# An attention and two-MLP kernel on one core: weight conversions on GpSimd's DMA queue, and new due times for VectorE and ScalarE

## The chip, the cores and the metric

The kernel runs on one core of a Trainium2 chip. The metric is the device time of one execution in microseconds. Three runs of the kernel before gave 1081.07, 1081.65 and 1086.11, so its median is 1081.65 us.

## The reference

Three layers, one behind the other; the second and third act on 1792 tokens of 768 values.

```
q, k, v: (4, 12, 448, 64) fp32
scores = q @ k.T / 8 - log(448);  attn = sigmoid(scores);  x = attn @ v   -> (1792, 768)
h = x @ w_in (768 x 2048, float64);   x = (h * cos(h)) @ w_out (2048 x 768, float64)
g = x @ w_gate; val = x @ w_val (768 x 1536, float64);  out = (silu(g) * val) @ w_out2
```

The weights arrive as float64 words. The kernel converts each 128 x 768 block to fp32 on the chip and keeps the result in a scratch buffer in DRAM (`swi`, `swo`, `swg`, `swv`, `swd`).

## The kernel before, in words

*Precision.* Every fp32 operand of a matmul is split into a high half (a rounded copy, made by ScalarE, sometimes by VectorE) and a low half (the difference, made by VectorE). Each product is three matmuls: high by high, high by low, low by high.

*Attention.* 24 pairs of heads run one after another. For each, VectorE splits q and k (L723, L724), TensorE makes four chunks of scores (24 matmuls, L734), ScalarE takes the sigmoid of each chunk out of PSUM (L738), and TensorE multiplies by v (16 matmuls, L748). ScalarE copies the result to `r` (L750). SP's queue loads `rqk` (q and k) and `vs` (v).

*The two MLPs.* The work is cut into 28 units: 16 of layer 1 (two halves of the tokens times eight blocks of 256 hidden values) and 12 of layer 2. A stage is one layer for one half of the tokens; units 0 to 7 are stage 0, 8 to 15 stage 1, 16 to 21 stage 2, 22 to 27 stage 3. An up product of a unit is done in seven block products of 9 matmuls, numbered 1 to 7 (`seven`, L1000), instead of eight, so the operands are sums and differences of blocks of x and of the weights, and the results are put together from PSUM banks by VectorE (`sum22`, `sum12`) and ScalarE (`first_copy`, `second_copy`, `fifth`). Layer 2 has two such products in a unit, gate and value. For layer 1, `h_cos_h` then makes a scaled copy and a rounded copy on ScalarE, takes their difference on VectorE (L816, the rounding step), the sine on ScalarE and the product on VectorE. `split_g` makes the two halves of g. Six down products of 12 matmuls (L902) follow, in the middle of the next unit's seven. At a stage's start the seven operands of x are made anew from `r` (`inputs`): a difference for four of them, a high half (L658 on ScalarE, L660 on VectorE) and a low half.

*Conversions.* One conversion loads the float64 words (`raw`, beside attention `lr`), and takes one or two ScalarE and four or five VectorE instructions; the result (`lt` beside attention, later `t` or `cv`) is stored. Four sets of buffers are lent to conversions while attention runs (`lend_pool`). All of these DMAs are issued by SP, in the order in which the planner gives them.

*What sets the order.* The order on TensorE is a string of tokens for each unit: a digit is a block product, d is a down product of the unit before. The order on the other engines is laid while the program is built, by a planner (`Order`). Each step says which engines can do it and how long it takes, and may carry a due time; the planner advances a clock, picks of the ready steps the one that can start first, and among equals the one with the smallest due time. Due times are the planned time of the product that needs the result, less a number of microseconds. Attention's own instructions are written in program order, and `beside` fills their gaps with planned steps. On the chip only the order is kept: each engine runs its list in sequence and waits on semaphores. Most VectorE and ScalarE instructions are recorded at the line of a helper (L230, L227).

Of the kernel before, what the change touches and what calls it, by code (L numbers as in the profile page):

```python
# [11 lines left out]
I32 = mybir.dt.int32  # L12
# [3 lines left out]
ALU = mybir.AluOpType  # L16
# [25 lines left out]
LATENCY = 0.15  # L42

# [30 lines left out]
class Order:  # L74
# [51 lines left out]
    def run(self, until=math.inf):  # L126
        while self.ready:
# [11 lines left out]
            (start, _), task, engine, time = best  # L139
            if start >= until:  # L140
                return
# [9 lines left out]
def block_kernel(  # L151
# [85 lines left out]

    LANDING = 5.0
    PAIR = 5.8
# [16 lines left out]
    PRODUCT = 0.203  # L256

    FIRST = ("1562734", "15627dd3dd4dd")
    ONE = ("1526dd7d3d4dd", "15d2d6d7d3d4d")
    TWO = "15d26d73d4"  # L260
    LAST = ('1526d734', '15d26d73d4dd')
# [116 lines left out]
    for n, (layer, _, c) in enumerate(units):  # L378
        for i in range(2):
# [4 lines left out]
            for w, key in of:  # L384
                uses.setdefault((id(w), 2 * c + i), due[key] - 25.0)
    todo = iter(todo)

    def lend_pool():
# [3 lines left out]
        for a in range(4):  # L392
# [3 lines left out]
            order.spawn(conversions(raw, t, backs[-1], stop), end)  # L396
# [11 lines left out]

    def absolute(t, words):
# [7 lines left out]
        return {"ACT": 0.9, "DVE": 0.58}, do  # L417

    def conversions(raw=None, t=None, back=None, stop=None):

        while not stop:
# [6 lines left out]
            yield move(raw.rearrange("p n two -> p (n two)"), flat(w[f]).bitcast(I32))  # L428
            yield LANDING
# [5 lines left out]
            yield by(time, ({"DVE": 0.56}, lambda _: nc.vector.tensor_scalar(  # L435
                t, t, HI_MOST, HI_LEAST, op0=ALU.min, op1=ALU.max
            )))
            yield {"DVE": 0.56}, lambda _: nc.vector.tensor_scalar(
                ti, ti, 3, 0x3FFFFFF8, op0=ALU.logical_shift_left, op1=ALU.bitwise_and
            ), time  # L440
            yield {"DVE": 0.96}, lambda _: nc.vector.scalar_tensor_tensor(
# [3 lines left out]
            yield by(time, vec(0.97, ti, ti, raw[:, :, 0], ADD))  # L445
# [4 lines left out]
            yield move(there[0], t)  # L450
# [55 lines left out]
    def operands():  # L506
# [16 lines left out]
        def lower(keys, s, t, lo, hi, size, room, free, done):  # L523
            yield by(due[keys[0]] - 1.2, vec(0.16 + size / 950, lo, t, f32(hi), SUB))
# [39 lines left out]
        def split(keys, t, free=None):  # L564
# [4 lines left out]
            yield by(due[keys[0]] - 2.4, copy(0.2 + size / 1200, hi, t))  # L569
# [19 lines left out]
        for n in range(n_units):  # L589
# [10 lines left out]
            for u in range(units[n][0]):  # L600
# [6 lines left out]
                yield combine(sums, a21, a22, ADD, due[n, u, 5] - 3.0)  # L607
                yield combine(a21, a11, a21, SUB, due[n, u, 7] - 3.0)
                last_sums = yield from split([(n, u, 5)], sums)
                yield first  # L610
                yield combine(a11, sums, a11, SUB, due[n, u, 6] - 4.0)
                yield combine(a12, a12, a11, SUB, due[n, u, 3] - 4.0)
# [32 lines left out]
    def inputs(s):  # L645
# [9 lines left out]
        def to_hi(out, t):  # L655
# [5 lines left out]
            return {"ACT": 1.32, "DVE": 0.9}, do  # L661
# [5 lines left out]
        def operand_of(i):  # L667
            t, parts = make[i]
            time = due[n, 0, i]
            if parts:  # L670
                for event in after[i]:
                    yield event
                yield by(time - 5.0, vec(1.6, t, parts[0], parts[1], SUB))
                made_t[i].set()
# [5 lines left out]
            yield by(time - 3.2, to_hi(hi, t))  # L680
# [443 lines left out]
```

## Time and profile before

| | |
|---|---|
| profiled execution | 1087.36 us |
| its span, first to last instruction | 1085.3 us |
| runs | 1081.07, 1081.65, 1086.11 us |
| TensorE matmuls busy | 1065.9 us (98%) |
| VectorE busy | 848.9 us (78%) |
| ScalarE busy | 664.8 us (61%) |
| GpSimd busy | 124.7 us (11%), 97 instructions |
| mean granted TensorE clock | 0.992 |

Busy shares are of the span. DMA issues are not counted as busy. Attention fills the span to about 154 us, layer 1 from there to about 600 us, layer 2 the rest. The profiled execution took 5.7 us more than the median of the runs.

### The profile page before, as it was taken

What the parts mean: (1) busy time and instruction counts of PE and PEld (TensorE: products, weight loads), DVE (VectorE), ACT (ScalarE), POOL (GpSimd) and SP (SyncE); (2) the same over time, 40 slices, a digit from 0 to 9 for tenths busy, and PEclk for the clock granted to TensorE, in tenths of its full rate; (3) what the DMA queues carried; (4) which work ended last, traced back from release to release, by engine and by line L of the source; (5) the groups of instructions that cost most, each with busy time, mean ns of one, the idle gap of its engine ahead of it and who ended that gap; (6) DMA issues with size and microseconds to landing.
All of it is one profiled execution on the core that took longest, in us unless ns stands there. A gap on an engine that the chain in (4) does not pass through costs nothing.

```text
span 1085.3 us, 14759 instructions
## 1 busy us (share of the span) xinstructions
PE 1065.9 (98%) x5507; PEld 933.1 (86%) x5507; DVE 848.9 (78%) x1138; ACT 664.8 (61%) x1005; POOL 124.7 (11%) x97
## 2 busy tenths in 40 slices
PE   9999999999999899999997999999999999999998
PEld 5554569999989799999997999999999999999997
DVE  4969759989999999989899888897559644555643
ACT  6887768877777777777776665554345344433330
POOL 0000002001111101100023100111111210110100
PEclk9999999999999899999998999999999999999999
DMA  9999424545654145454513565655122322112002
GB/s 267 301 264 248 143 88 146 200 150 175 220 202 146 59 161 205 160 188 146 189 59 122 170 221 202 203 189 175 45 73 76 117 85 73 56 48 73 30 1 102
DMA packets 64455, 156.68 MB, mean 144 GB/s; under 512 B 10112, under 2 KB 36736, under 8 KB 64384
## 3 DMA queue, kind: packets, MB, share of 16 engines
q1 hardware_dynamic: 64240, 155.51, 45.3%
q8 instruction: 43, 0.70, 0.3%
q10 hardware_dynamic: 144, 0.23, 0.1%
q14 instruction: 28, 0.23, 0.1%
HBM read 123.47 MB, written 32.24 MB: 143 GB/s over the span
## 4 chain that ended last, share of the span: by engine, by line
PE 88%; DVE 9%; issue 1%; ACT 1%; DMA 0%; DVEq 0%; ACTq 0%
PE banks L1000 42%; PE banks L902 33%; PE banks L748 7%; PE banks L734 6%; DVE x L230 2%; DVE r L230 2%; DVE u L230 1%; DVE g L230 1%; DVE wa L230 1%; DVE wb L230 0%; DMA rqk<-in_qk 0%; DVE u L816 0%; DVE s L230 0%; DVE x L660 0%; ACT x L658 0%
## 5 line engine op out<-in xcount | busy, mean ns | idle before, releaser
L902 PE MATMUL banks<-g,wb 128*128 128x448 f32 x1044 | 224.2, 362 | 1.1 <-ACT g L227 0.6
L1000 PE MATMUL banks<-x,wb 128*128 128x448 f32 x1044 | 224.9, 363 | 0.3 <-ACT banks L227 0.3
L902 PEld LDWEIGHTS banks<-g,wb 128*128 128x128 f32 x1044 | 195.5, 187 | 15.5 <-ACT g L227 1.4
L1000 PEld LDWEIGHTS banks<-x,wb 128*128 128x128 f32 x1044 | 196.8, 189 | 14.0 <-ACT banks L227 0.7
L902 PE MATMUL banks<-g,wa 128*128 128x448 f32 x720 | 160.6, 370 | 9.8 <-ACT g L227 8.5
L1000 PE MATMUL banks<-x,wa 128*128 128x448 f32 x738 | 159.7, 362 | 0.1
L902 PEld LDWEIGHTS banks<-g,wa 128*128 128x128 f32 x720 | 137.9, 192 | 21.3 <-ACT g L227 9.3
L1000 PEld LDWEIGHTS banks<-x,wa 128*128 128x128 f32 x738 | 138.2, 187 | 10.3 <-issue 0.7
L227 ACT ACTIVATE u<-u 128x448 f32<-128x448 f32 x179 | 99.4, 570 | 39.4 <-DVE u L230 26.6
L230 DVE TENSOR_TENSOR u<-u,banks 128x448 f32<-128x448 f32 x119 | 73.4, 617 | 57.1 <-PE banks L1000 54.1
L230 DVE TENSOR_TENSOR r<-banks,r 128x896 f32<-128x896 f32 (+1 forms) x69 | 74.2, 1075 | 50.5 <-PE banks L902 50.0
L738 ACT ACTIVATE a<-banks 128x896 f32<-128x896 f32 x96 | 82.9, 920 | 20.2 <-PE banks L734 12.4
L230 DVE TENSOR_TENSOR wb<-t,wb 128x768 fp32r<-128x768 f32 x73 | 69.5, 956 | 14.9 <-ACT wb L227 14.4
L227 ACT ACTIVATE g<-u 128x448 fp32r<-128x448 f32 x97 | 55.1, 572 | 39.0 <-DVE u L230 23.9
L1000 PE MATMUL banks<-x,s 128*128 128x448 f32 x360 | 78.5, 362 | 0.0
L734 PEld LDWEIGHTS banks<-qk 64*128 64x128 f32 x576 | 51.5, 188 | 29.6 <-ACT a L738 8.2
L227 ACT ACTIVATE wb<-t 128x768 fp32r<-128x768 f32 x73 | 60.9, 837 | 24.6 <-PE banks L1000 17.8
L512 POOL TENSOR_TENSOR sum<-t 128x384 f32<-128x384 f32 x20 | 35.2, 1758 | 339.9 <-DMA t<-swi 78.1
L734 PE MATMUL banks<-qk 64*128 64x448 f32 x576 | 69.9, 386 | 3.5 <-ACT a L738 2.2
L227 ACT ACTIVATE r<-banks 128x896 f32<-128x896 f32 x52 | 47.8, 920 | 41.1 <-PE banks L902 41.0
L1000 PEld LDWEIGHTS banks<-x,s 128*128 128x128 f32 x360 | 67.5, 188 | 4.5
L227 ACT ACTIVATE banks<-banks 128x448 f32<-128x448 f32 x80 | 42.3, 529 | 46.3 <-PE banks L1000 45.1
(103 smaller groups left out, 1476.3 us busy)
## 6 DMA issues: line engine op xcount, KB each, us to landing
raw<-in_w_out SPq DMA_DIRECT2D x23, 768.0 KB, 5.2
t<-swi SPq DMA_DIRECT2D x32, 384.0 KB, 3.2
t<-swo SPq DMA_DIRECT2D x64, 192.0 KB, 2.5
rqk<-in_qk SPq DMA_DIRECT2D x47, 224.0 KB, 7.5
raw<-in_w_gate SPq DMA_DIRECT2D x12, 768.0 KB, 4.6
raw<-in_w_val SPq DMA_DIRECT2D x12, 768.0 KB, 4.9
t<-swg SPq DMA_DIRECT2D x18, 384.0 KB, 3.0
t<-swd SPq DMA_DIRECT2D x34, 192.0 KB, 3.0
```

The lines of the kernel that those rows point to most:

```text
L227: return {"ACT": time}, lambda _: nc.scalar.activation(**kw)
L230: return {"DVE": time}, lambda _: nc.vector.tensor_tensor(out=out, in0=in0, in1=in1, op=op)
L512: on.tensor_tensor(out=out, in0=a, in1=b, op=op)
L734: nc.tensor.matmul(sc[:, j], lhsT=both[half, m, 1, starts[c]:starts[c] + P], rhs=both[half, p, 0], start=n == 0, stop=n == 2,)
L738: nc.scalar.activation(out=a, in_=sc, func=AF.Sigmoid, bias=-math.log(S), scale=1.0 / math.sqrt(D))
L748: nc.tensor.matmul(o[half], lhsT=value, rhs=a[:, j], start=c == 0, stop=c == NCH)
L902: nc.tensor.matmul(banks[:, first + e - d, :N], lhsT=w[:, m, e % KH, :], rhs=g[:, 1 - p], start=(i, m, p) == (0, 0, 0) and is_fresh and no ...
L1000: nc.tensor.matmul(bank, lhsT=w[:, m, k, :], rhs=x[p][:, k], start=(k, m, p) == (0, 0, 0) and i in (1, 5), stop=(k, m) == (KH - 1, 1), ski ...
```

## The change

Beside attention, the raw weights are loaded and the converted ones stored by GpSimd's queue (`move_beside`) instead of SP's. Each of the four lent conversions first waits a planned 6.0 + 4.5 a microseconds (a from 0 to 3), and then for a one-column copy on GpSimd that reads the q and k of pair a + 1, so that its first load is issued behind those. The planner allows 9.5 us for landing there instead of 5.0.

All leads before due times stand in one table now, with new values; the planned durations of the conversions, of the low halves and of the x casts on VectorE (0.9 to 1.55) are new, and a VectorE step that starts while GpSimd is planned busy counts 1.12 times its duration. The token strings of layer 2 (TWO) and of the last unit (LAST) differ; those of layer 1 do not.

```diff
+LEAD = {
...
+    "ghi": -2.87,
+    "glo": -2.34,
...
+    "xlo": -11.72,
...
+            if engine == "DVE" and self.busy.get("POOL", 0.0) > start:
+                time *= 1.12
...
+    def move_beside(out, in_):
+        return {"POOL": 0.9}, lambda _: nc.gpsimd.dma_start(out=out, in_=in_)
+
     LANDING = 5.0
+    LANDING_BESIDE = 9.5
...
-    TWO = "15d26d73d4"
-    LAST = ('1526d734', '15d26d73d4dd')
+    TWO = '1526dd7d34'
+    LAST = ('1562734d', '1d5627dd3dd4')
...
+    def begun(a, raw_qk, steps):
+
+        yield 6.0 + 4.5 * a
+        yield {"POOL": 0.3}, lambda _: nc.gpsimd.tensor_copy(warm[:, a:a + 1], raw_qk[:, (a + 1) % 4, 1, S - 1:S])
+        yield from steps
...
-            yield move(raw.rearrange("p n two -> p (n two)"), flat(w[f]).bitcast(I32))
-            yield LANDING
+            convey = move_beside if back else move
+            yield convey(raw.rearrange("p n two -> p (n two)"), flat(w[f]).bitcast(I32))
+            yield LANDING_BESIDE if back else LANDING
...
-            yield by(due[keys[0]] - 1.2, vec(0.16 + size / 950, lo, t, f32(hi), SUB))
+            yield by(due[keys[0]] - LEAD["wlo"], vec(0.25 + size / 1080, lo, t, f32(hi), SUB))
...
-            return {"ACT": 1.32, "DVE": 0.9}, do
+            return {"ACT": 1.32, "DVE": 1.55}, do
...
-            yield by(time - 1.7, vec(1.6, lo, t, f32(hi), SUB))
+            yield by(time - LEAD["xlo"], vec(1.6, lo, t, f32(hi), SUB))
...
-        yield by(time - 1.5, copy(0.6, g[:, 1], f))
-        yield by(time - 0.8, vec(0.65, g[:, 0], f, f32(g[:, 1]), SUB))
+        yield by(time - LEAD["ghi"], copy(0.6, g[:, 1], f))
+        yield by(time - LEAD["glo"], vec(0.65, g[:, 0], f, f32(g[:, 1]), SUB))
...
```

Three places in the order. First VectorE at the end of unit 15, the last of layer 1. Before, from the accumulation behind `sum12` on: `r1<-banks` is that accumulation, `x1<-r0` low halves of the next stage's operand, `r0<-r0` a difference for it, L816 the rounding step of unit 15.

```order
L230 TENSOR_TENSOR r1_65<-banks_63,r1_65 128x896
L230 TENSOR_TENSOR x1_1325<-r0_64,x1_1325 128x3x448 x2
L230 TENSOR_TENSOR r0_64<-r0_64 128x1344
L816 SCALAR_TENSOR_TENSOR u0_1440<-u5_1449,u0_1440 128x448
L230 TENSOR_TENSOR x1_1325<-t3_1450,x1_1325 128x768
L230 TENSOR_TENSOR wb2_1448<-t_66,wb2_1448 128x768
L816 SCALAR_TENSOR_TENSOR u2_1442<-u5_1449,u2_1442 128x448
L230 TENSOR_TENSOR wa0_68<-t_66,wa0_68 128x768
```

The same place now, from `sum12` (the first row) on; L858 is the rounding step, `g3<-u1` and `g1<-u4` are the low halves of g for the first down product.

```order
L261 TENSOR_TENSOR u1_1436<-u1_1436,u0_1435 128x448
L858 SCALAR_TENSOR_TENSOR u4_1439<-u5_1444,u4_1439 128x448
L261 TENSOR_TENSOR x0_72<-r0_64,x0_72 128x3x448
L261 TENSOR_TENSOR u3_1438<-u3_1438,banks_63 128x448
L261 TENSOR_TENSOR r0_64<-r0_64 128x1344
L261 TENSOR_TENSOR u4_1439<-u4_1439,u2_1437 128x448
L261 TENSOR_TENSOR wb2_1443<-t_66,wb2_1443 128x768
L261 TENSOR_TENSOR g3_1434<-u1_1436,g3_1434 128x448
L261 TENSOR_TENSOR r0_64<-r0_64 128x1344
L261 TENSOR_TENSOR wa0_68<-t_66,wa0_68 128x768
L261 TENSOR_TENSOR g1_1432<-u4_1439,g1_1432 128x448
L261 TENSOR_TENSOR x0_72<-r0_64,x0_72 128x3x448
```

The rounding step and the halves of g moved ahead of low halves of x; those stand behind g now.

Second, VectorE in the middle of layer 1, behind the seven of unit 4. Before, with L816 the rounding steps of groups (1, 1), (0, 1) and (1, 0) of unit 4, and `wa1` the low half of a weight pair.

```order
L816 SCALAR_TENSOR_TENSOR u1_1441<-u5_1449,u1_1441 128x448
L230 ISA t_66<-raw1_1434,t_66 128x1536
L816 SCALAR_TENSOR_TENSOR u0_1440<-u5_1449,u0_1440 128x448
L230 TENSOR_TENSOR u1_1441<-u1_1441,u4_1444 128x448
L816 SCALAR_TENSOR_TENSOR u2_1442<-u5_1449,u2_1442 128x448
L414 TENSOR_SCALAR cv_1435<-raw0_1433 128x768
```

The same place now, from the rounding step of group (0, 1) to that of group (1, 0); `wa1` and `wa0` are low halves of weight pairs.

```order
L858 SCALAR_TENSOR_TENSOR u2_1437<-u5_1444,u2_1437 128x448
L261 TENSOR_TENSOR wa1_69<-t3_1445,wa1_69 128x768
L261 TENSOR_TENSOR g0_1431<-u0_1435,g0_1431 128x448
L261 TENSOR_TENSOR wa0_68<-t_66,wa0_68 128x768
L858 SCALAR_TENSOR_TENSOR u4_1439<-u5_1444,u4_1439 128x448
```

Two low halves of weights and a low half of g moved between the two rounding steps.

Third, the DMAs beside attention. Before, on SP's queue: `lr` are raw weights, `swi0<-lt0` the store of a converted block, `rqk` and `vs` the inputs of attention.

```order
L236 DMA lr3_120<-in_w_in 128x1536
L707 DMA rqk_79<-in_qk 64x2x448 x2
L708 DMA vs4_165<-in_v 128x384
L716 DMA t_66<-in_v 64x3x64 x2
L707 DMA rqk_79<-in_qk 64x2x448 x2
L708 DMA vs5_217<-in_v 128x384
L236 DMA swi0_261<-lt0_115 128x768
L707 DMA rqk_79<-in_qk 64x2x448 x2
```

On GpSimd's queue now, with the one-column copies (L447).

```order
L447 COPY warm_71<-rqk_79 128x1
L270 DMA lr3_120<-in_w_in 128x1536
L270 DMA swi0_313<-lt0_115 128x768
L270 DMA lr0_114<-in_w_out 128x1536
L270 DMA swi1_381<-lt1_117 128x768
L270 DMA lr1_116<-in_w_out 128x1536
```

SP's queue keeps `rqk`, `vs` and the loads of converted weights; the loads of raw weights and the stores beside attention moved to GpSimd's.

## Rows read from the trace of the kernel before

**Rows 1.** The chain that ended last, shares of the span by engine.
```profile
PE 88%; DVE 9%; issue 1%; ACT 1%; DMA 0%; DVEq 0%; ACTq 0%
```
**Rows 2.** TensorE's waits: engine, line, releaser: us in total, times, longest.
```profile
PE banks L902 <- ACT g L227: 9.1, 3, 5.7
PE banks L734 <- ACT a L738: 2.2, 1, 2.2
```
**Rows 3.** A window: us, busy time of each engine, granted clock, DMA share, GB/s.
```profile
365.20:371.80 6.60, 6.01 (x15) 5.00 (x16) 5.21 (x7) 3.27 (x6) 2.00 (x1) 0.50 0.55 173
```
**Rows 4.** The chain in order of time, layer 1: start us, us, what.
```profile
275.37 7.20 PE banks L1000 x36
...
392.49 7.20 PE banks L1000 x36
```
**Rows 5.** Timeline of TensorE in attention: start us, us, engine, line, operation, [idle before].
```profile
91.11 2.48 PE L748 MATMUL banks<-a,vs 128*64 128x448 f32 x12
...
104.48 0.87 PE L734 MATMUL banks<-qk 64*128 64x448 f32 x6 [2.19 <-ACT a L738]
105.28 4.17 PE L748 MATMUL banks<-a,vs 128*64 128x448 f32 x12
```
**Rows 6.** Timeline of TensorE at the switch from stage 0 to stage 1.
```profile
365.19 0.74 PE L902 MATMUL banks<-g,wa 128*128 128x448 f32 x1 [2.80 <-ACT g L227]
366.52 4.47 PE L902 MATMUL banks<-g,wa 128*128 128x448 f32 x11 [0.59 <-DVE g L230]
```
**Rows 7.** Timeline of TensorE at the switch from layer 1 to layer 2.
```profile
572.65 2.56 PE L902 MATMUL banks<-g,wb 128*128 128x448 f32 x12
...
583.45 1.97 PE L1000 MATMUL banks<-x,s 128*128 128x448 f32 x9
...
600.27 1.36 PE L902 MATMUL banks<-g,wa 128*128 128x448 f32 x6
```
**Rows 8.** Timeline of VectorE at the switch from layer 1 to layer 2.
```profile
574.63 0.61 DVE L230 TENSOR_TENSOR u<-u,banks 128x448 f32<-128x448 f32 x1
575.16 1.55 DVE L230 TENSOR_TENSOR x<-r,x 128x1344 fp32r<-128x1344 f32 x1
576.63 1.08 DVE L230 TENSOR_TENSOR r<-banks,r 128x896 f32<-128x896 f32 x1
577.63 3.01 DVE L230 TENSOR_TENSOR x<-r,x 128x1344 fp32r<-128x1344 f32 x2
...
582.03 0.61 DVE L816 SCALAR_TENSOR_TENSOR u<-u,u 128x448 f32<-128x448 f32 x1
...
583.44 0.95 DVE L230 TENSOR_TENSOR wb<-t,wb 128x768 fp32r<-128x768 f32 x1
...
591.25 0.61 DVE L230 TENSOR_TENSOR g<-u,g 128x448 fp32r<-128x448 f32 x1
```
**Rows 9.** Timeline of ScalarE in attention.
```profile
92.19 0.92 ACT L738 ACTIVATE a<-banks 128x896 f32<-128x896 f32 x1 [0.32 <-PE banks L748]
...
101.86 1.32 ACT L658 ACTIVATE x<-r 128x1344 fp32r<-128x1344 f32 x1 [2.84 <-DVE r L230]
```
**Rows 10.** Timeline of VectorE in attention.
```profile
74.92 0.63 DVE L723 CAST qk<-rqk 128x896 fp32r<-128x896 f32 x1 [3.93 <-DMA rqk<-in_qk]
```
**Rows 11.** Timeline of VectorE and TensorE behind unit 4.
```profile
282.39 0.62 DVE L230 TENSOR_TENSOR g<-u,g 128x448 fp32r<-128x448 f32 x1
282.41 3.78 PE L902 MATMUL banks<-g,wb 128*128 128x448 f32 x18
```
**Rows 12.** DMA issues to 130 us: count, KB each, median us to landing.
```profile
rqk<-in_qk SPq DMA_DIRECT2D x47, 224.0 KB, 7.5
lr<-in_w_in SPq DMA_DIRECT2D x8, 768.0 KB, 9.7
```
**Rows 13.** Timeline of GpSimd at the switch from layer 1 to layer 2.
```profile
588.35 6.66 POOL L512 TENSOR_TENSOR sum<-t 128x384 f32<-128x384 f32 x1 [17.93 <-DVE u L816]
```
**Rows 14.** A group of the page's part 5: busy us, mean ns, idle before.
```profile
L512 POOL TENSOR_TENSOR sum<-t 128x384 f32<-128x384 f32 x20 | 35.2, 1758 | 339.9 <-DMA t<-swi 78.1
```

More of the change, by code (lines that the diff above doesn't have):

```diff
@@ L42 @@
 LATENCY = 0.15
+LEAD = {
+    "u": 6.41,
+    "f": 3.86,
+    "stt": 4.78,
+    "sin": 3.9,
+    "mult": 4.38,
+    "ghi": -2.87,
+    "glo": -2.34,
+    "whi": 17.07,
+    "wlo": 7.63,
+    "c5": 3.74,
+    "c7": -12,
+    "c6": -0.3,
+    "c3": -12,
+    "xd": 4.51,
+    "xhi": 11.35,
+    "xlo": -11.72,
+    "sv": -9.73,
+    "acc": -11.08,
+    "bank": -3.13,
+    "first": -1.99,
+    "second": 1.43,
+    "fifth": -1.94,
+    "s22": 4.84,
+    "s12": 4.53,
+    "silu": -12,
+    "conv": 19.63,
+}
 class Event:
@@ L395, in lend_pool @@
             backs.append(order.event())
-            order.spawn(conversions(raw, t, backs[-1], stop), end)
+            order.spawn(begun(a, raw_qk, conversions(raw, t, backs[-1], stop)), end)
         def swap():
@@ L444, in conversions @@
             ), time
-            yield by(time, vec(0.97, ti, ti, raw[:, :, 0], ADD))
+            yield by(time, vec(1.0, ti, ti, raw[:, :, 0], ADD))
             if not back:
@@ L449, in conversions @@
             there[0] = dram.tile([P, KD * P], F32, tag=f"s{names[id(w)]}{f}", name=f"s{names[id(w)]}{f}")
-            yield move(there[0], t)
+            yield convey(there[0], t)
             order.spawn(landed(there[1], None if back else t), 0)
@@ L764, in attention @@
             split(0)
-            stops = [lend_pool()]
+            stops = [lend_pool(raw_qk)]
             for i in range(NPAIR):
@@ L846, in accumulate @@
         two, acc = banks[:, first:first + 2, :N], R[h][:, j, d:d + 2]
-        time = after_down(n, j, d) - 1.3
+        time = after_down(n, j, d) - LEAD["acc"]
         if place[n, j, d] == len(down_steps) - 1:
@@ L876, in banker @@
                     acc = R[units[n][1]][:, j, d:d + 2]
-                    yield by(due["down", n, j, d] - 1.3, copy(0.92, banks[:, first:first + 2, :N], acc))
+                    yield by(due["down", n, j, d] - LEAD["bank"], copy(0.92, banks[:, first:first + 2, :N], acc))
                 held[j, d] = first
@@ L968, in after @@
                     z[ij] = ((yield tmps), order.event())
-                order.spawn(silu(z[ij][0], h, read, z[ij][1], min(time, due["g", n, key[2]] - 6.0)), 0)
+                order.spawn(silu(z[ij][0], h, read, z[ij][1], min(time, due["g", n, key[2]] - LEAD["silu"])), 0)
             else:
```

54 lines of the change are left out of this document (27 added, 27 removed).

## The prediction

> **What bounds the kernel now.** I read the chain that ended last first [rows 1]. Its shares by engine are to be read as one statement: 88% is TensorE's own matmuls, so the kernel is a TensorE stream and only what interrupts that stream costs time. Then TensorE's waits [rows 2]: the matmuls of the down products (L902) wait for ScalarE's half of g, 9.1 us in 3 waits, the longest 5.7; attention's scores (L734) wait once, 2.2 us. Waits alone are not the price, since the granted clock falls after a long one: it stands at 0.50 (1.2 GHz instead of 2.4) in the stretch behind the wait at 365 us [rows 3]. So I price each interruption by the position of the products behind it.
>
> From 572.65 to 583.45 TensorE runs 54 matmuls (12 + 9 + 24 + 9) in 10.80 us without a wait: 0.200 us a matmul [rows 7], and 27.0 us for the 135 of a whole unit of layer 1.
> - A, attention at 102 us: 2.19 us idle, then 16 matmuls in 4.17 us where twelve of them normally take 2.48 [rows 5]: 2.19 + 1.69 = 3.9 us.
> - B, units 4 to 7: from 275.37 to 392.49 are 117.12 us for four units of 27.0, so 9.1 us lost [rows 4]. Of these the switch from stage 0 to stage 1 takes 2.80 + 0.59 idle, 4.47 - 11 x 0.2 = 2.3 at half clock, and about 0.5 to the end of that stretch: 6.2 us [rows 3, 6]. The other 2.9 us lie inside units.
> - C, the switch from layer 1 to layer 2: from 583.45 to 600.27 are 16.82 us for 9 + 12 + 18 = 39 matmuls, 7.8 us undisturbed: 9.0 us lost [rows 7].
>
> Together 22.0 us. With the profiled execution at 1087.36 us, a stream without any of it would take 1065.3.
>
> **Why those waits are there.** C first. Between the last sum of unit 15 (574.63) and the first rounding step of its h cos h (582.03) VectorE does three low halves of the next stage's operand x (one, then two in 3.01 us), an accumulation and a difference for x; the last low half of g that TensorE waits for starts at 591.25 [rows 8]. The work of the next stage stands ahead of the work that TensorE needs first. B's switch has the same form. A is a ScalarE cast of a stage operand that sits in front of the next pair's sigmoids and waits 2.84 us for a VectorE difference [rows 9]; VectorE was late because it had waited for q and k, 3.93 us in front of 74.92 [rows 10].
>
> **The change part by part.** *Stage switches.* The order shows, for unit 15, the rounding step directly behind the sum, and low halves of x behind it. I add up the rows from that sum to the last low half of g that the first down product reads, with durations start to start from the same stretch (u or g step 0.53, x step 1.47, accumulation 1.00, and 0.87 for the low half of a weight pair, which is what 582.03 to 583.44 leaves behind a u step [rows 8]): 19 rows and 16.6 us before, 14 rows and 11.7 us after, 4.9 us less; for unit 7, 16 rows and 13.7 us before, 11 rows and 9.0 us after, 4.7 us less. At unit 7 the wait was 3.4 us, so it goes. At unit 15 the wait was 5.7 us, so 0.8 would stay; but layer 2's new token string puts two more products (18 x 0.2 = 3.6 us) in front of the first down product of unit 15, so it goes too. What is late next is product 6 of unit 16: its low half of x moves from 1 row behind the sum to 15 rows, 13.2 us. TensorE has 14.4 us of products between (one down, product 4, two downs, products 1, 5, 2), and in the trace the sum started 2.0 us behind the end of product 3 (574.63 against 572.65, where the next down product began [rows 7, 8]): 14.4 - 2.0 - 13.2 = -0.8, so a wait of 0.8, bounds 0 to 1.5. Gain 6.2 + 9.0 - 0.8 = 14.4 us.
>
> *Inside the units.* VectorE's order there hardly changes in length: over the 16 units of layer 1 the rows from the last sum to g's last low half of group (1, 0) are 295 before and 291 after. One place gets worse. In unit 4 the rounding step of that group falls behind both low halves of a weight pair: 7.9 us of rows ahead of it become 9.7, and the low half of g comes 0.9 to 1.7 us later. Before, that low half started at 282.39 and the down product at 282.41 [rows 11], so there is no margin to speak of. I take 1.5 us of new wait and keep the 2.9 us. Bounds: 0, if the finer spacing also removes the old 2.9, to 9, if each of three such places costs 3 with its stretch at half clock. The waits of 2.19 and 2.80 us had stretches at half clock behind them [rows 3, 5, 6]; whether one of 1.5 has, no row shows, and that lies in these bounds.
>
> *Attention.* 12 conversions instead of 13 run beside it; their 12 loads and 12 stores leave SP's queue for GpSimd's. On SP a load of q and k no longer stands behind a store that waits for VectorE. Before, q and k took 7.5 us at the median and the raw weights 9.7 in one queue [rows 12]. The cast that made A has the same form after: it stands behind the last sigmoid of pair 14 and needs the VectorE difference behind the split of pair 15. Its slot opens when that sigmoid ends, at about 93.1 before [rows 9]. Back from there over VectorE's rows after: difference 1.5, split 1.6, two x steps 2.9, split 1.6, four conversion steps and a cast 4.2, split 1.6, conversion steps 3.2, split 1.6, so the split of pair 12 has to start by about 74.9; before it started at 74.92 and had waited 3.93 us for q and k [rows 10]. With these loads out of the weights' way it should start earlier, so A goes: 3.9 us, bounds 0 to 3.9. The planner also counts VectorE's x casts at 1.55 us instead of 0.9, which is what an x step of that size takes [rows 8].
>
> What GpSimd's queue costs is not in this trace: no DMA is issued there. From below it is nothing; from above, one GpSimd addition took 6.66 us beside a busy VectorE, while its group's mean is 1.76 [rows 13, 14]. 24 issues are 42 us at the mean, or 160 us at the worst, in some 120 us. I take the mean, the nearest thing to an issue whose writes share time with VectorE: hidden, since the first cast of raw weights stands behind the sigmoids of pair 2 now and of pair 1 before, and the loads keep the margin that 9.7 us of landing had there. If that cover is gone, rival 2 gives the price.
>
> The Trainium skill speaks against this edit: "SBUF — State Buffer", section "SBUF: two separate sides", says that a DMA issued from GpSimd's queue needs GpSimd to write its descriptors, and that VectorE in a two-port mode locks it out until its instruction ends. By that rule an issue waits at most for one VectorE instruction at a time; the 6.66 us row agrees that GpSimd can be held off, and no run so far shows a descriptor held off.
>
> *Rest.* 11 weight sums move from VectorE to GpSimd (89 to 100 there), 19 us at 1.76 [rows 14]; VectorE gives up about 11 x 0.53 = 6 us over 900, off the path. Layer 2's and the end's new strings keep every matmul; layer 2 ran without waits worth naming before, so I cost them at nothing, with VectorE's idle time there as cover.
>
> **Sum.** 1087.36 - 3.9 - 14.4 + 1.5 = 1070.6 for an execution like the profiled one. The median of the runs is 1081.65, 5.7 below it, and the runs reach from 1081.07 to 1086.11. If they lose less to the same waits, the new kernel is near 1070; if the gap is one of the measurement, at 1064.9. I take 1068.
>
> **Rivals.** (1) *The waits move into the units.* The copies of g are now 4.4 and 3.1 us less urgent. If 8 of 16 units each lose 1.5 us, the sum is 12 - 1.5 = 10.5 higher than mine, 1078 to 1081: no change. For it: VectorE's load and the missing margin at 282.4; against it: the row counts are level.
>
> (2) *GpSimd's queue is too slow, slower than before.* Place: the casts of raw weights that ScalarE does once per pair, in order, in front of the sigmoids; a late load stops the scores. Price: 24 issues of t us must fit into 120. From t = 5.0 on, what exceeds it lands on TensorE; 14 us of gain are eaten at t = 5.6 and at 6.66 the kernel takes about 1107. For it: the 6.66 row. Against it: the 1.76 mean. A milder form, first weights late by 20 us in all, gives 1088. (3) *Attention is not mended*, because the same cast waits for the same kind of difference: 1072. Against it: the earlier q and k.
>
> **How the numbers follow.** Half a per cent (5.4 us) is about what a measurement of this kernel can tell from no change: faster means under 1076.2. Forecast with the waits at the switches gone: 0.62 around 1068, own range 1063 to 1073; rival 3 about 0.14, also faster; rival 1 0.14, mostly no change; rival 2 0.10, slower. So 0.76 faster, 0.14 the same, 0.10 slower. The range ends at 1062, below 1064.9 by the 2.9 us that may also go, and at 1079, inside rival 1.
>
> **What would show it.** Right: TensorE's timeline gapless around 365 and 591 us, no granted clock of 0.50 there, and the rounding step of unit 15 directly behind its sum; in attention no wait of L734's successor for ScalarE, and VectorE's waits for q and k below 3 us. Wrong: waits of about 1 to 2 us for g in many units of layer 1, a wait in front of product 6 behind the switch above 2 us, or ScalarE's cast of raw weights waiting for a DMA in attention.

## The result and the profile after

Four runs of the changed kernel took 1069.14, 1069.96, 1070.30 and 1070.52 us, a median of 1070.13; the kernel before stands at 1081.62 over four. The ratio is 0.9883 with a 95% interval of 0.9856 to 0.9911: faster by 1.2%. The prediction said 1068 and gave 1062 to 1079. The profiled execution took 1069.14 us, with a span of 1067.4.

The chain that ended last, in the kernel after, shares of the span by engine:

```profile
PE 92%; DVE 5%; issue 1%; ACT 1%; DMA 0%; DVEq 0%; ACTq 0%
```

Against [rows 1], 4% of the span went from VectorE to TensorE in that chain. TensorE's waits in the kernel after (engine, line, releaser: us in total, times, longest; L1042 is the line of the block products now, L944 that of the down products, L776 of the scores):

```profile
PE banks L1042 <- DVE x L261: 1.4, 1, 1.4
...
PE banks L1042 <- ACT banks L258: 1.1, 2, 0.8
PE banks L944 <- ACT g L258: 0.6, 1, 0.6
...
PE banks L944 <- ACT banks L258: 0.4, 1, 0.4
...
PE banks L944 <- DVE g L261: 0.4, 1, 0.4
```

The 9.1 us for ScalarE's half of g [rows 2] are 0.6, and attention's wait for a sigmoid is no longer listed. All that is left behind attention is 1.4 + 1.1 + 0.6 + 0.4 + 0.4 = 3.9 us. Added to the prediction's undisturbed stream of 1065.3 that makes 1069.2; the profiled execution took 1069.14. Its first score matmuls, which this sum leaves out, also ended 1.2 us earlier than before, so the agreement is good to about a microsecond and no better. These are the main places, from TensorE's timeline after (start us, us, ..., [idle before]); 0.79, 0.43 and 0.33 us for banks at 170.11, 349.62 and 815.15 are the rest:

```profile
279.55 0.47 PE L944 MATMUL banks<-g,wb 128*128 128x448 f32 x1 [0.56 <-ACT g L258]
280.39 3.08 PE L944 MATMUL banks<-g,wb 128*128 128x448 f32 x14 [0.37 <-DVE g L261]
...
578.62 1.88 PE L1042 MATMUL banks<-x,wa 128*128 128x448 f32 x8 [1.39 <-DVE x L261]
```

279.55 is unit 4's down product, for which 1.5 us were predicted (0.56 + 0.37 = 0.93 came); 578.62 is product 6 of unit 16 (0.8 predicted, 1.39 came). Where [rows 3] had a granted clock of 0.50, both switches now stand at 1.00; the first down product of unit 7 starts at 358.14 us without a wait. Windows of the kernel after (us, busy time by engine, clock, DMA share, GB/s):

```profile
356.00:366.00 10.00, 10.00 (x52) 9.37 (x51) 9.99 (x11) 9.04 (x13) 2.32 (x2) 1.00 0.38 118
572.00:592.00 20.00, 18.61 (x93) 16.85 (x92) 20.00 (x21) 13.23 (x20) 9.82 (x4) 1.00 0.12 41
```

VectorE at the switch from layer 1 to layer 2, to be read against [rows 8]:

```profile
564.73 0.61 DVE L261 TENSOR_TENSOR u<-u,banks 128x448 f32<-128x448 f32 x1
565.26 0.61 DVE L858 SCALAR_TENSOR_TENSOR u<-u,u 128x448 f32<-128x448 f32 x1
...
576.49 0.60 DVE L261 TENSOR_TENSOR g<-u,g 128x448 fp32r<-128x448 f32 x1
577.02 1.54 DVE L261 TENSOR_TENSOR x<-r,x 128x1344 fp32r<-128x1344 f32 x1
...
580.49 0.60 DVE L261 TENSOR_TENSOR u<-u,banks 128x448 f32<-128x448 f32 x1
```

The last sum of unit 15 (`sum12`) starts at 564.73 and the rounding step right behind it; the order list in "The change" starts four rows later, with a multiplication and not with `sum12`. The second low half of g is made at 576.49, 11.8 us behind the sum, where it was 591.25 - 574.63 = 16.6 [rows 8]; the prediction's rows gave 11.7. One low half of x (568.74) still stands in between, where there were four; the others come behind. The row at 580.49 turned out to matter as much: it is the multiplication of unit 15's group (1, 0), the last reader of a PSUM bank.

Attention, ScalarE's cast of an x operand and VectorE's split of pair 12 in the kernel after, against [rows 9, 10]: neither waits for a DMA or a difference now.

```profile
91.50 1.32 ACT L700 ACTIVATE x<-r 128x1344 fp32r<-128x1344 f32 x1
```
```profile
70.08 0.63 DVE L765 CAST qk<-rqk 128x896 fp32r<-128x896 f32 x1 [1.24 <-PE banks L776]
```

DMA issues to 130 us in the kernel after, against [rows 12] (count, KB each, median us to landing), and one of GpSimd's issues from its timeline:

```profile
rqk<-in_qk SPq DMA_DIRECT2D x47, 224.0 KB, 8.7
lr<-in_w_in POOLq DMA_DIRECT2D x8, 768.0 KB, 10.2
```
```profile
27.70 0.84 POOL L270 DMA_DIRECT2D swi<-lt  x1 [4.07 <-DVE lt L261]
```

An issue takes under a microsecond. q and k land later after their issue than before, 8.7 against 7.5 us, and VectorE waits for them about as long. Its waits to 150 us, before and after (us in total, times, longest):

```profile
DVE qk L723 <- DMA rqk<-in_qk: 17.8, 6, 5.0
```
```profile
DVE qk L765 <- DMA rqk<-in_qk: 16.4, 8, 5.0
```

### The profile page after: what moved, and what is told of

Read it like the earlier page. It is cut to its first block, busy times and chain, and to the rows that moved or that the text cites. A ratio compares the mean times of both kernels' runs of the same rounds, so it can differ in the third digit from the quotient of the medians.

```text
span 1067.4 us, 14771 instructions
## 1 busy us (share of the span) xinstructions
PE 1057.6 (99%) x5507; PEld 926.8 (87%) x5507; DVE 849.9 (80%) x1121; ACT 669.5 (63%) x1011; POOL 167.5 (16%) x136
## 4 chain that ended last, share of the span: by engine, by line
PE 92%; DVE 5%; issue 1%; ACT 1%; DMA 0%; DVEq 0%; ACTq 0%
PE banks L1042 43%; PE banks L944 36%; PE banks L790 7%; PE banks L776 6%; DVE x L261 1%; DVE r L261 1%; DVE wa L261 1%; DVE u L261 0%; DMA rqk<-in_qk 0%; DVE g L261 0%; ACT x L700 0%; DVE wb L261 0%; DVE u L858 0%; DVE s L261 0%; ACT banks L258 0%
## 5 line engine op out<-in xcount | busy, mean ns | idle before, releaser
L944 PE MATMUL banks<-g,wb 128*128 128x448 f32 x1044 | 225.1, 362 | 0.9 <-ACT g L258 0.6
L1042 PE MATMUL banks<-x,wb 128*128 128x448 f32 x1044 | 224.3, 362 | 0.3 <-ACT banks L258 0.3
L944 PEld LDWEIGHTS banks<-g,wb 128*128 128x128 f32 x1044 | 195.6, 187 | 14.6 <-ACT g L258 0.9
L1042 PE MATMUL banks<-x,wa 128*128 128x448 f32 x954 | 205.5, 362 | 2.2 <-DVE x L261 1.4
L1042 PEld LDWEIGHTS banks<-x,wb 128*128 128x128 f32 x1044 | 195.6, 187 | 14.0 <-ACT banks L258 1.0
L1042 PEld LDWEIGHTS banks<-x,wa 128*128 128x128 f32 x954 | 178.6, 187 | 15.9 <-DVE x L261 1.8
L944 PE MATMUL banks<-g,x 128*128 128x448 f32 x540 | 115.8, 362 | 0.0
L261 DVE TENSOR_TENSOR r<-banks,r 128x896 f32<-128x896 f32 (+1 forms) x69 | 74.1, 1075 | 45.6 <-PE banks L944 45.2
L944 PEld LDWEIGHTS banks<-g,x 128*128 128x128 f32 x540 | 101.2, 187 | 6.8
L258 ACT ACTIVATE g<-u 128x448 fp32r<-128x448 f32 x102 | 58.2, 575 | 62.9 <-DVE u L261 52.6
L944 PE MATMUL banks<-g,wa 128*128 128x448 f32 x432 | 93.2, 363 | 0.6 <-ACT banks L258 0.4
L944 PEld LDWEIGHTS banks<-g,wa 128*128 128x128 f32 x432 | 80.6, 188 | 7.5 <-ACT banks L258 1.7
L261 DVE TENSOR_TENSOR wb<-t,wb 128x768 fp32r<-128x768 f32 x72 | 73.8, 1028 | 13.0 <-ACT wb L258 12.4
L1042 PE MATMUL banks<-x,s 128*128 128x448 f32 x360 | 78.5, 362 | 0.0
L261 DVE TENSOR_TENSOR g<-u,g 128x448 fp32r<-128x448 f32 x102 | 69.1, 685 | 9.0 <-ACT g L258 8.7
L776 PEld LDWEIGHTS banks<-qk 64*128 64x128 f32 x576 | 50.3, 185 | 27.3 <-ACT lr L258 7.7
```

Of the source, the lines that this page charges most:

```text
L258: return {"ACT": time}, lambda _: nc.scalar.activation(**kw)
L261: return {"DVE": time}, lambda _: nc.vector.tensor_tensor(out=out, in0=in0, in1=in1, op=op)
L776: nc.tensor.matmul(sc[:, j], lhsT=both[half, m, 1, starts[c]:starts[c] + P], rhs=both[half, p, 0], start=n == 0, stop=n == 2,)
L944: nc.tensor.matmul(banks[:, first + e - d, :N], lhsT=w[:, m, e % KH, :], rhs=g[:, 1 - p], start=(i, m, p) == (0, 0, 0) and is_fresh and no ...
L1042: nc.tensor.matmul(bank, lhsT=w[:, m, k, :], rhs=x[p][:, k], start=(k, m, p) == (0, 0, 0) and i in (1, 5), stop=(k, m) == (KH - 1, 1), ski ...
```

## The experiments

The theory at the start was the prediction's: the gain is made at the two stage switches by what stands ahead of g on VectorE, and in attention by the queue. "Before" took 1082.8 to 1083.8 us at the median beside these runs, each ratio is against it.

**e1, one number alone.** The kernel before with the due time of the low halves of x changed.

```diff
-            yield by(time - 1.7, vec(1.6, lo, t, f32(hi), SUB))
+            yield by(time + 11.72, vec(1.6, lo, t, f32(hi), SUB))
```

> The kernel before with one number changed: the due time of the low halves of x, from 1.7 us ahead of the product to 11.72 us behind it. Counted in VectorE's order, the second half of g for the first down product of unit 7 stands 12 rows behind sum12 instead of 16, and that of unit 15 stands 20 rows behind it instead of 19. Theory (what stands between the sum and g on VectorE sets the switch waits): the switch from stage 0 to stage 1 loses its 6.2 us, the one from layer 1 to layer 2 keeps its 9.0, attention keeps its 3.9; so 1081.6 - 6.2 = about 1075.5, with a wait of 5 us or more for g behind unit 15. Rival 1 (this number alone makes the gain): both switches without waits, about 1068 to 1071. Rival 2 (the gain comes from GpSimd's queue or from the token strings): 1081 to 1082.

Measured 1084.73, ratio 1.0016 (1.0003 to 1.0029): no gain. TensorE's timeline of it, from unit 6's down products to unit 7's:

```profile
336.69 0.74 PE L902 MATMUL banks<-g,wa 128*128 128x448 f32 x1 [2.83 <-ACT g L227]
339.30 5.01 PE L902 MATMUL banks<-g,wa 128*128 128x448 f32 x14 [1.86 <-DVE g L230]
...
363.95 2.56 PE L902 MATMUL banks<-g,wa 128*128 128x448 f32 x12
```

At the switch to stage 1 (363.95) the wait is gone, as the theory said. But the down products of unit 6, one unit ahead, now wait 2.83 + 1.86 us and start slowly, where the kernel before waited 0.69. The wait at the switch to layer 2 stayed, 4.43 + 0.59, and 3 us of new waits for weights, x and g stood in layer 2. The theory was right about the place and missed the time by 9 us.

**e4, the number put back.** The kernel after with `"xlo": 1.7`.

> The kernel after with one number put back: the due time of the low halves of x at 1.7 us ahead of the product. In VectorE's order the second half of g stands 11 rows behind sum12 in unit 7, as after, but 24 rows in unit 15 (14 after, 19 before), with five low halves of x ahead of it. Theory: the switch to stage 1 stays mended; the one to layer 2 waits again, 5.7 us plus 5 rows of some 0.9 us less the 3.6 us of the two products that the new string puts ahead of the down product, 6 to 7 us of wait and up to 3 more for half clock: 1070.1 + 6 to 10 = 1076 to 1080. Rival (the waits went by the new string or by other leads): 1070.

Measured 1094.43, ratio 1.0107 (1.0083 to 1.0130), 14 us over the upper end expected. Its longest waits, from TensorE's timeline, at the switch to layer 2 and at the one from stage 2 to stage 3:

```profile
590.33 3.73 PE L1042 MATMUL banks<-x,wb 128*128 128x448 f32 x9 [7.21 <-ACT banks L258]
...
841.92 0.74 PE L944 MATMUL banks<-g,x 128*128 128x448 f32 x1 [6.11 <-ACT g L258]
```

Two more waits for banks, 3.50 and 2.14 us, stand at 354 and 574 us. The switch to stage 1 stayed mended (unit 7's down product starts at 364.54 without a wait). So that switch has no wait with this number alone (e1) nor with all but this number (e4), while the later ones need it in the order laid here. And the 7.21 us are not for g: TensorE waits for a PSUM bank that ScalarE has to write. The theory had no term for that, nor for the switch to stage 3.

**e2, the queue alone, planned anew.** The kernel before with `move_beside`, `begun` and the landing of 9.5; leads, durations and strings as before.

> The kernel before with only the move of attention's conversions to GpSimd's queue, their spacing included; all leads, durations and strings as before. Theory: attention's wait of 2.2 us and its slow stretch go (3.9 us), the two switches keep theirs, since VectorE's order there is the same within one row; so 1081.6 - 3.9 = about 1077.7. Rival (the queue makes most of the gain, through earlier converted weights later on): about 1070. Rival (the queue gives nothing by itself, attention is mended by the order of VectorE and ScalarE): 1081 to 1082.

Measured 1090.67, ratio 1.0067 (1.0048 to 1.0086). No wait in attention behind 10 us, but 5.47 us at the switch to stage 1, 5.73 at the one to layer 2 as before, and a new 1.89 at 227 us.

**e3, all but the queue, planned anew.** The kernel after with SP, a landing of 5.0 and no spacing.

> The kernel after with attention's conversions back on SP's queue and without the spacing; leads, durations and strings as after. The second half of g stands 12 rows behind sum12 in unit 7 and 10 in unit 15, as near as in the kernel after (11 and 14). Theory: the switches stay mended and attention's loss of 3.9 us comes back, so about 1074. Rival (the queue makes most of the gain): 1079 to 1082. Rival (the queue gives nothing): 1070.

Measured 1087.55, ratio 1.0038 (1.0025 to 1.0051), 17 us above the kernel after, and none of its waits in attention or at the two switches. They are, inside the units:

```profile
PE banks L944 <- ACT banks L258: 5.0, 2, 2.8
PE banks L944 <- ACT g L258: 4.2, 3, 3.2
PE banks L944 <- DVE g L261: 3.4, 3, 1.3
PE banks L1042 <- ACT banks L258: 2.0, 2, 1.7
```

All four runs changed the order far behind the place of the edit, since the planner lays everything anew from there. So the next ones hold the order.

**f1 and f2, the queue with the order held.** First (f1) the kernel after, issued by SP in the order of after; then (f2) the kernel before, issued by GpSimd in the order of before.

```diff
-        return {"POOL": 0.9}, lambda _: nc.gpsimd.dma_start(out=out, in_=in_)
+        return {"POOL": 0.9}, lambda _: nc.sync.dma_start(out=out, in_=in_)
```
```diff
+    def move_beside(out, in_):
+        return {"SP": 0.8}, lambda _: nc.gpsimd.dma_start(out=out, in_=in_)
```

> The kernel after with every engine's order held as it is; only the loads and stores of attention's conversions are issued by SP instead of GpSimd, at the same places of the plan. It tells the queue itself from the new order that the planner lays when it is told of another queue (which e3 changed too). Theory (the queue keeps q and k early): a store on SP holds back the loads of q and k again, attention stalls as before for 2.2 us with a slow stretch, 1070.1 + 3.9 = 1074; the rest stays mended. Rival 1 (the order of VectorE and ScalarE decides; e3 and e4 have no stall at 100 us, with and without the queue): 1070, within 1. Rival 2 (the transfers themselves cost e3 its 17 us): 1084 or more.

> The kernel before with every engine's order held; only the loads and stores of attention's conversions are issued by GpSimd instead of SP. Theory (the queue mends attention): the wait of 2.2 us at 104 us and its slow stretch go, all waits behind 300 us stay as they were; 1082.8 - 3.9 = about 1079. Rival 1 (the order decides): the wait stays, 1082 to 1083. Rival 2 (transfers from GpSimd's queue disturb others; e2 took 1090.7): 1088 or more, with the waits of e2 at 227 and 369 us.

The first took 1069.64, ratio 0.9866 (0.9848 to 0.9883): as the kernel after, with the same waits (1.4, 1.1, 0.6, 0.4, 0.4). The queue is worth nothing that these runs can tell in the new order, and the 17.9 us between f1 and e3, which use the same queue, are the planner's: for e3 it was told of other landings and starts, without the spacing, and laid a worse order. (In f1, q and k landed 7.9 us after their issue, the raw weights 9.3 instead of 10.2.) The second took 1090.39, ratio 1.0054 (1.0038 to 1.0070). TensorE's timeline of it, near the start:

```profile
17.38 0.74 PE L738 MATMUL banks<-qk 64*128 64x448 f32 x2 [5.26 <-DVE qk L727]
```
VectorE's split of the second pair before, then in this run, and GpSimd in this run:
```profile
8.14 0.63 DVE L723 CAST qk<-rqk 128x896 fp32r<-128x896 f32 x1 [0.75 <-DMA rqk<-in_qk]
```
```profile
16.60 0.63 DVE L727 CAST qk<-rqk 128x896 fp32r<-128x896 f32 x1 [9.01 <-DMA rqk<-in_qk]
```
```profile
1.30 2.25 POOL L239 DMA_DIRECT2D lr<-in_w_in  x4 [0.45 <-issue]
```

Without the spacing GpSimd issues four raw weights from 1.30 us on; before, SP issued the same four from 9.76 us on, behind seven loads of q and k. VectorE then waits 9.01 us for q and k of the second pair and has them 8.5 us later than before, though SP issues them from 2.32 us on in both. In e2, which has the spacing in an order laid anew, no such wait stood there (TensorE's 46 score matmuls ran from 7.47 us without one). So the spacing undoes a cost that the queue brings at the start. The Trainium skill, "DMA: Bandwidth & Descriptors", section "Queues, rings and completion order", says that each DMA engine takes turns between the queues that have work; the 9.01 us agree. The wait of 2.19 us in attention [rows 5] is gone in f2, as its theory said, but TensorE also reaches those scores 9 us later (109.11 us), so this doesn't show that the queue mended it. The median landing of q and k was 5.7 us here: which queue lands them sooner depends on the order around them.

**f3, the switch to layer 2, order held up to unit 15.** The kernel before; the low halves of x for products 7, 3 and 4 of unit 16 and the difference for 4 wait for the halves of g.

```diff
+            if s == 2 and i in (7, 3, 4):
+                for k in range(2):
+                    yield g_ready[n - 1, k, 1]
             yield by(time - 1.7, vec(1.6, lo, t, f32(hi), SUB))
```

> The kernel before; at the switch from layer 1 to layer 2 alone, the low halves of x for products 7, 3 and 4 and the difference for product 4 wait until the halves of g for the first down product of unit 15 are made. All engines' order up to unit 15 is that of before, so attention and the switch to stage 1 keep their losses. The second half of g stands 14 rows behind sum12 instead of 19, without four steps of x of 1.47 us. Theory (what stands in front of g on VectorE is the cause of the wait): the 5.7 us at 591 us and the half clock behind them go, 1082.8 - 9.0 = about 1074. Rival (the wait only moves to the products of x, as e4's 7.2 us in front of a product at 590 us suggests): 1079 to 1083, with waits in front of products 7, 3 or 4 of unit 16.

Measured 1083.98, ratio 1.0001 (0.9985 to 1.0016): the rival. The wait for g, before and in f3, and another that came in front of product 7, from TensorE's timelines:

```profile
591.15 5.25 PE L902 MATMUL banks<-g,wa 128*128 128x448 f32 x12 [5.73 <-ACT g L227]
```
```profile
584.50 2.48 PE L908 MATMUL banks<-g,wa 128*128 128x448 f32 x11 [0.22 <-DVE g L230]
...
596.93 3.73 PE L1006 MATMUL banks<-x,wa 128*128 128x448 f32 x9 [3.95 <-ACT banks L227]
```
What it waits for, on ScalarE and on VectorE of the same run:
```profile
596.35 0.53 ACT L227 ACTIVATE banks<-banks 128x448 f32<-128x448 f32 x1 [1.75 <-DVE u L230]
```
```profile
588.16 1.55 DVE L230 TENSOR_TENSOR r<-r 128x1344 f32<-128x1344 f32 x1
...
592.10 1.55 DVE L230 TENSOR_TENSOR x<-r,x 128x1344 fp32r<-128x1344 f32 x1
...
595.71 0.61 DVE L230 TENSOR_TENSOR u<-u,banks 128x448 f32<-128x448 f32 x1
```
The same multiplication before:
```profile
596.43 0.61 DVE L230 TENSOR_TENSOR u<-u,banks 128x448 f32<-128x448 f32 x1
```

ScalarE's copy into product 7's bank waits for the multiplication at 595.71, which reads group (1, 0) of unit 15 out of that bank, and that stands behind five steps of x now (three low halves, a difference and a cast, from 584.36 to 592.10). The new theory: two chains leave the last unit of a stage through VectorE, g for the down products and the last read of a bank, and what stands ahead of either stops TensorE. In the kernel before the second was late too (596.43, where product 7, at 602.67, would have come 9.0 us earlier without the wait for g), hidden behind the first.

**f5, both chains.** As f3, but only product 7's low half waits for g; the difference for 4 and the low half for 3 wait for that multiplication.

```diff
+            if s == 2 and i in (7, 3):
+                yield g_ready[n - 1, 0, 1] if i == 7 else unread
...
+        if key == (15, 1, 0):
+            unread.set()
```

> The kernel before, order held up to unit 15, as in f3; but now only the low half of x for product 7 waits for the halves of g of the first down product, and the difference for product 4 and the low half for product 3 wait for the multiplication of group (1, 0) of unit 15, the last reader of the PSUM bank that ScalarE's copy in front of product 7 writes. In f3 that multiplication came at 595.71 us behind four steps of x, and product 7 waited 3.95 us. Here it stands 21 rows behind sum12 instead of 25, with no further step of x ahead of it: about 588.8 us, in time for product 7 at 592.8. Theory (two chains leave unit 15 through VectorE, g and this bank, and what stands ahead of either stops TensorE): neither wait stays, 1083.8 - 9.0 = about 1075. Rival (the waits move on to product 3 or 4, whose halves of x are later now): 1079 or more.

Measured 1077.96, ratio 0.9953 (0.9937 to 0.9969). TensorE's timeline before, then of f5; the first two rows of each are product 1 of unit 16's gate and product 1 of its value, with 99 matmuls between them (19.8 us undisturbed):

```profile
581.65 1.96 PE L1000 MATMUL banks<-x,wb 128*128 128x448 f32 x9
...
610.47 1.96 PE L1000 MATMUL banks<-x,wb 128*128 128x448 f32 x9
```
```profile
582.82 1.96 PE L1007 MATMUL banks<-x,wb 128*128 128x448 f32 x9
...
603.12 1.96 PE L1007 MATMUL banks<-x,wb 128*128 128x448 f32 x9
...
712.18 0.68 PE L1007 MATMUL banks<-x,wb 128*128 128x448 f32 x2 [2.10 <-ACT wb L227]
```

Product 7 begins at 595.32 without a wait, and of the waits at this switch 0.22 us for g are left. From product 1 to product 1 are 20.3 us, before 28.8: the switch gave 8.5 us, where 9.0 were predicted. The run stays 3 us above the expected 1075; a new wait for weights, 2.10 + 0.46 us at 712 us, in the part of layer 2 that the planner laid anew, is of that size. The profiled execution, at 1084.47, is 6.5 us above the median of its twelve runs; *The level* below says where most of that may lie.

**f4, the token string alone.** The kernel before with layer 2's new string.

```diff
-    TWO = "15d26d73d4"
+    TWO = '1526dd7d34'
```

> The kernel before with layer 2's new token string alone, which puts products 2 and 6 ahead of the first down product of unit 15. The second half of g stands 18 rows behind sum12 (19 before), the multiplication of group (1, 0) 23 rows (24 before). Theory of the prediction (only g counts): the 5.73 us wait loses 3.6 and a row, about 1.3 us stay and the half clock goes, 1083.8 - 7 = about 1077. Theory of two chains: product 7 comes at about 595.2 us and the copy into its bank is not written before 596.5 to 601, so 1 to 5 us of wait in front of product 7 take the place of the wait for g: 1078 to 1083.

Measured 1080.44, ratio 0.9968 (0.9955 to 0.9981), within the second theory's range; the bank that was late was another, in front of product 2. TensorE's timeline of it:

```profile
576.72 1.96 PE L1000 MATMUL banks<-x,wb 128*128 128x448 f32 x9
...
584.91 3.50 PE L1000 MATMUL banks<-x,wb 128*128 128x448 f32 x9 [4.42 <-ACT banks L227]
...
602.81 1.96 PE L1000 MATMUL banks<-x,wb 128*128 128x448 f32 x9
```

From product 1 to product 1 are 26.1 us, 2.7 less than before, and the medians differ by 2.9. The string is worth that, by itself.

**f6, both switches.** f5 with the same holding back for unit 7 too (`s in (1, 2)`, and an event for each).

> The kernel before with the same holding back as in f5, now at the switch from stage 0 to stage 1 as well (low half of x for product 7 behind the halves of g of the first down product of unit 7, product 3's and the difference for product 4 behind the multiplication of group (1, 0) of unit 7). Two low halves of x leave the stretch between sum12 and g, 2.9 us; but the planner fills it with five steps of conversions (four of about 0.5 us, one of 0.95), and the second half of g stands 18 rows behind sum12 instead of 16. Theory (the time of all that stands ahead of g counts, whatever it is): the switch to stage 1 keeps its wait of 2.8 us and half clock, and the whole comes out as f5, 1078, give or take what a newly laid stage 1 costs. Rival (the steps of x alone are the cause): both switches are mended, f5 less 6.2 = about 1072.

Measured 1083.26, ratio 1.0002 (0.9985 to 1.0019). Neither expectation met it. The first switch got better, 1.73 + 0.86 us and full clock behind it; but stage 1 was laid anew from there, and the second switch waits again, 3.55 + 0.97, with 2.7 us in layer 2. What one place gains the next order loses.

**g1 and g2, the rest of the waits.** (g1) The kernel after with a due time of its own for the low half of x for product 6 at the switch; then also (g2) for the difference for product 4.

```diff
-            yield by(time - LEAD["xlo"], vec(1.6, lo, t, f32(hi), SUB))
+            lead = -4 if (s, i) == (2, 6) else LEAD["xlo"]
+            yield by(time - lead, vec(1.6, lo, t, f32(hi), SUB))
```
```diff
-                yield by(time - LEAD["xd"], vec(1.6, t, parts[0], parts[1], SUB))
+                yield by(time - (-8 if (s, i) == (2, 4) else LEAD["xd"]), vec(1.6, t, parts[0], parts[1], SUB))
```

> The kernel after; the low half of x for product 6 at the switch to layer 2 has its due time 4 us ahead of the general one for low halves of x counted from the product (4 us behind the product instead of 11.72). It then stands 12 rows behind sum12 instead of 15, where the difference for product 4 stood; g stays at 14 rows. The order up to there is that of after. Theory (the 1.39 us in front of product 6 is that low half's place): the wait goes and nothing is late in its stead, 1070.1 - 1.4 = 1068.7. Rival (the planner lays layer 2 anew from there and new waits come): 1070 to 1073.

> The kernel after with the low half of x for product 6 at its earlier place as in g1, and the difference for product 4 with a later due time (8 us behind the product instead of 4.51 ahead): it stands behind the multiplication of group (1, 0) now, which stands 17 rows behind sum12 instead of 18 (20 in g1). Theory of two chains: neither the 1.39 us in front of product 6 nor g1's 1.85 us in front of product 7 is there, and layer 2 starts 1.4 us earlier: 1069.6 - 1.4 = about 1068.3. Rival (product 4, whose high and low halves come later, waits instead; or new waits deeper in layer 2): 1070 or more.

1071.08, ratio 0.9880 (0.9860 to 0.9900), and 1070.70, ratio 0.9877 (0.9858 to 0.9897): no difference from the kernel after that these runs can tell. In the first the 1.39 us are gone and 1.85 us stand in front of product 7, whose multiplication moved from 580.49 to 582.76: the second chain again. In the second both are gone, and 0.18 + 0.45 + 0.71 us came at 590, 742 and 754 us. No version beat the kernel after by more than these runs can tell.

## Why the prediction was right, and where it was not

- *What bounds the kernel, and the sum.* Right. The undisturbed stream of 1065.3 and what is left of waits give the profiled time to about a microsecond. Without a long wait no stretch at half clock is left (mean granted clock 1.000, before 0.992), as the pricing by positions assumed.
- *The switches, 6.2 + 9.0.* The size was right: both waits and their slow stretches are gone. The first gave 6.7 us in the kernel after (unit 6's last six matmuls to product 6 of unit 8, 357.43 to 375.52 before and 353.34 to 364.74 after); the second was measured at 8.5 by itself in f5, and gave 7.2 in the kernel after (21.7 us from product 1 to product 1), where 9.0 - 0.8 were predicted. The reason was half of it. "What is late next is product 6" left out the PSUM banks: moving x behind g alone gained nothing (1083.98), moving it behind g and behind the last reading of the bank gained 5.4 us at the medians (1077.96). The first switch lost its wait both in e1, by the due time of x's low halves alone, and in e4, without it; which of the steps the kernel after owes it to is open.
- *The token string.* It was put at what was left of a wait, 0.8 us; alone it gives 2.7, and it needs the banks in time as well.
- *Product 6, 0.8 us.* It came to 1.39, inside its bounds of 0 to 1.5. Of the terms of that sum one was off: unit 15's last sum started 3.2 us behind the end of product 3 (564.73 against 561.55), not 2.0.
- *Inside the units.* 1.5 us for unit 4 came to 0.93: its first three matmuls, from 278.22 us on, ran ahead of the wait, a margin that the prediction didn't count. The old waits for g in units 5 and 6 are gone; in their place stand 0.79 at 170 us and 0.43 at 349, both for a bank, which was not foreseen. Over the four units of B, less the switch, the sum kept 2.9 + 1.5 us; 2.5 were lost (271.02 to 381.54, less 108).
- *Attention, 3.9 us by the queue.* This step failed. q and k were to come earlier because the weights leave their queue. In the kernel after they are in time for pair 12 (70.08), but on the whole they land 8.7 us after their issue instead of 7.5, and VectorE's longest wait for them is 5.0 us as before, where the prediction's sign of being right was below 3. The stall is gone, but with SP's queue and the new order (f1, pair 12 split at 69.41) it is gone too, and the order of before doesn't always have it. f4 has attention's order unchanged, and its TensorE reaches the scores that stalled in [rows 5] at 100.18 us, as before; there pair 12 is split at 71.80 us, 28.4 ahead, and the cast doesn't wait. VectorE's and ScalarE's timelines of that run:

```profile
71.80 0.63 DVE L723 CAST qk<-rqk 128x896 fp32r<-128x896 f32 x1 [3.37 <-DMA rqk<-in_qk]
```
```profile
98.92 1.32 ACT L658 ACTIVATE x<-r 128x1344 fp32r<-128x1344 f32 x1
```

  Four more profiled executions have the same order here. In f3 the split came 25.7 us ahead of those scores (73.60 against 99.28), and they stalled for 1.80 us; in f5 25.3 and 2.18; in [rows 5, 10] 25.3 and 2.19 (74.92 against 100.18); in f6 27.4 (73.37 against 100.80), and they did not stall. So the limit lies between 25.7 and 27.4 us, where the prediction's 74.9 had put it at 25.3, and whether the split makes it varies from one execution to the next. What in the new order brings it to 28.6 (70.08 against 98.68) was not taken apart.
- *The level.* The stall may explain most of the 5.7 us between the profiled execution and the median that the prediction left open. Unit 5's wait for g, the same place of the same order, before and in f4:

```profile
306.56 0.47 PE L902 MATMUL banks<-g,wb 128*128 128x448 f32 x1 [0.56 <-ACT g L227]
```
```profile
302.52 0.47 PE L902 MATMUL banks<-g,wb 128*128 128x448 f32 x1 [0.57 <-ACT g L227]
```

  It stood at 305.25 and 307.93 in f3 and f5, which stalled, and at 303.34 in f6, which did not: 2 to 5 us lie between executions with the stall and without, 4.0 between the first profile and f4. The profiled executions of f4 and f6 also lie below their medians (by 1.1 and 0.5 us), those of the kernel before, f3 and f5 above (by 5.7, 1.2 and 6.5). That the ordinary runs mostly escape the stall fits this, but they left no trace, so it is not shown. It would be the branch for which the prediction had named 1070. It took 1068 between two branches, and 1070.13 came.
- *GpSimd's queue.* Costed at nothing, rightly, though at 1.76 us an issue where 0.53 to 0.89 came. Rival 2 had no ground in the new order: with all DMAs back on SP the time was the same. In the old order the queue did cost 6.6 us (f2), by what it let start early, not by slow issues. The rule that the prediction weighed (the Trainium skill, "SBUF — State Buffer", section "SBUF: two separate sides") would hold an issue until VectorE's instruction ends; none of the 24 issues beside attention took over 0.89 us. The raw weights landed 0.9 us later than from SP in the same order (f1), at no cost in time, so the rule cost nothing that these runs show.
- *Rival 1, waits inside the units,* did not come in the kernel after, but it came in e3's order: 5.0 + 4.2 + 3.4 + 2.0 = 14.6 us of waits with the same leads. It was a matter of the order laid, not of g's copies being less urgent.

## What to carry to other kernels

Where a planner lays the order, undoing one part of a change tests another order, not that part: hold the order and swap only what the hardware does, or hold everything up to the place in question. Name a wait by its place in the string of products and not by its time: e1's wait at 337 us stands a unit ahead of the switch that e1 mended. At a stage switch list every chain that leaves the last unit, operands and PSUM banks both, since mending the one that waits now uncovers the next. And look whether a wait of the profiled execution stands in other executions of the same order before its price goes into a sum against a median.

## What the runs showed of the hardware

GpSimd's additions and VectorE's steps can take longer beside each other. GpSimd's and VectorE's timelines of the kernel after at the switch to layer 2:

```profile
576.74 4.71 POOL L554 TENSOR_TENSOR sum<-t 128x384 f32<-128x384 f32 x1 [15.69 <-DMA t<-swv]
...
583.22 2.22 POOL L554 TENSOR_TENSOR t<-sum,t 128x384 f32<-128x384 f32 x1
```
```profile
582.19 2.37 DVE L261 TENSOR_TENSOR x<-r,x 128x1344 fp32r<-128x1344 f32 x1
```

Two additions of the same size take 4.71 and 2.22 us, and a low half of x 2.37 beside the second, but 1.54 beside the first (577.02). Attention's first 46 score matmuls took 5.79 to 5.82 us in five of the profiled executions and 6.55 to 7.49 in eight; six of these eight had a granted clock of 1.00 throughout, f4 and f5 0.71 from 7.00 to 12.80 us. Why was not tried.
